# Four heads at a time in 64x64 tiles of TensorE, one ring for all of PSUM, and products of two batches mixed

## The chip, the core and the metric

The kernel runs on one core of a Trainium2 chip. A core has five engines that work side by side, each through its own list of instructions in order: TensorE (PE: matrix products, and the loads of their weights, PEld), VectorE (DVE), ScalarE (ACT), GpSimd (POOL, which here mostly issues loads) and SyncE (SP, which issues stores and transposing copies). They wait for each other through semaphores. TensorE writes its results to PSUM, a memory of eight banks; a bank holds 512 float32 values in each of 128 partitions. ScalarE and VectorE carry them on to SBUF. The time is the device time of one execution in microseconds (us).

## The reference, cut to what matters

Relu-squared attention over 12 heads, then an MLP mixer: a product across tokens, and a two-layer product across channels.

```python
# q, k, v: (8, 12, 448, 64) float32
scores = (1 / 8) * q @ k^T
attn   = maximum(scores, 0) ** 2 / 448 @ v            # (8, 12, 448, 64)
x      = attn as (8, 448, 768)
h      = maximum(x^T @ w_tok1, 0) @ w_tok2            # (448, 256), (256, 448)
u      = x + h^T
h2     = maximum(u @ w_ch1, 0) @ w_ch2                # (768, 1536), (1536, 768)
out    = u + h2                                       # (8, 448, 768) float32
```

## The kernel before

A step works on one pair of heads (48 steps). The heads' 64 channels lie one above the other in 128 partitions, so that a score product uses a 64-row half of the array and a value product a 64-column half. 448 keys are three blocks of 128 and a rest of 64; the two rests of a pair go through one zero-padded 128x128 product. Products with channels are put in a queue and poured between the steps.

```python
ps_att = tile_pool(bufs=2, PSUM)       # two slots of two banks: scores
ps_acc = tile_pool(bufs=1, PSUM)       # one bank: values
ps_mm  = tile_pool(bufs=3, PSUM)       # three banks: everything else

def transposes(s):
    ps = ps_mm.tile([128, 1024], BF16, tag="bank", name="qkT_ps")
    ...                                # 16 transposes: q by 112, k by 128, the rest kz
    nc.vector.tensor_copy(sb, ps[:, : KO + KM + 128])

def scores(s, blocks):
    for c in blocks:
        ps = ps_att.tile([128, 2, 512], FP32, tag="att", name="sc_ps")
        for e in range(2):             # one matmul for each head of the pair
            h = slice(64 * e, 64 * (e + 1))
            nc.tensor.matmul(ps[:, e, :S], lhsT=sb[h, KO + c * 128 : KO + (c + 1) * 128],
                             rhs=sb[h, :S], start=True, stop=True)
    ...                                # relu on ScalarE (at), square on VectorE (sq)

def values(s):                         # 6 matmuls on column halves; values_rest adds one of 128x128
    ...
def values_rest(s):
    ...
    nc.vector.tensor_scalar(out=xT[b % 2][:, p, :S], in0=ps[:, :S], scalar1=float(alpha2), ...)

def token2(s):
    ps = ps_mm.tile([128, 512], FP32, tag="bank", name="h_ps")
    ...                                # 2 matmuls of 448 columns
    nc.vector.tensor_tensor(out=uT_tiles[b // 2][:, p, off : off + S],
                            in0=ps[:, :S], in1=xT[b % 2][:, p, :S], op=ALU.add)

def channel1(b, e):
    ps = ps_mm.tile([128, 512], FP32, tag="bank", name="m1_ps")
    ...                                # 6 matmuls of 448 columns
    nc.scalar.activation(r2[:, e, off : off + S], ps[:, :S], AF.Relu)

def channel2(bb, t, half):
    ps = ps_mm.tile([128, 512], FP32, tag="bank", name="m2_ps")
    for e in range(EC):                # 12 matmuls of 384 columns
        nc.tensor.matmul(ps[:, :HN], lhsT=r2[:, e, tok], rhs=wc2[:, e, cols], ...)
    nc.vector.tensor_tensor(out=o[:, cols], in0=ps[:, :HN], in1=u_tiles[bb][...], op=ALU.add)
    ...                                # after half 1: stores to out

for s in range(NS + 4):
    scores(s, (0, 1)); load_pair(s + 3); ...
    transposes(s + 1)
    values(s - 1)
    scores(s, (2,))
    values_rest(s - 1); ...
    square(); fill(0.25); scores_rest(s); x_back(s - 2); fill(0.25); square()
    ...                                # token2, token1 every second step, fill(0.25) after each
```

`x_back` brings the attention result into token-major order: by transposes on TensorE in the first 12 steps, by a transposing copy afterwards. `token1` is 8 matmuls of 256 columns for two pairs. `fill` pours channel work from the queue, a quarter of a step's share each time.

Of the kernel before, what the change touches and what calls it, by code (L numbers as in the profile page):

```python
# [16 lines left out]
def kernel(  # L17
# [18 lines left out]
    NP = H // 2  # L36
    QC = 4
    QP = S // QC
    KB = 3
    KM = KB * 128  # L40
    KR = S - KM
# [3 lines left out]
    SP = 512  # L45
    HN = DM // 2
    NT = 2 * S // 128

# [4 lines left out]
    raw = ctx.enter_context(tc.tile_pool(name="raw", bufs=6))  # L53
# [3 lines left out]
    ps_att = ctx.enter_context(tc.tile_pool(name="ps_att", bufs=2, space=bass.MemoryType.PSUM))  # L57
    ps_acc = ctx.enter_context(tc.tile_pool(name="ps_acc", bufs=1, space=bass.MemoryType.PSUM))
    ps_mm = ctx.enter_context(tc.tile_pool(name="ps_mm", bufs=3, space=bass.MemoryType.PSUM))
# [4 lines left out]
    kz = [consts.tile([128, NP, 128], BF16, name=f"kz{i}") for i in range(2)]  # L64
    vz = [consts.tile([128, NP, 128], BF16, name=f"vz{i}") for i in range(2)]
    xT = [consts.tile([128, NP, SP], BF16, name=f"xT{i}") for i in range(2)]
# [5 lines left out]


    raws = {}

    def load_pair(s):
        b, p = divmod(s, NP)
        h0 = 2 * p
        q_raw = raw.tile([QP, 2, QC, D], BF16, name="q_raw")
        k_raw = raw.tile([128, 2, KB, D], BF16, name="k_raw")  # L80
        v_raw = raw.tile([128, 2, KB, D], BF16, name="v_raw")
        nc.gpsimd.dma_start(  # L82
            out=q_raw.rearrange("p h c d -> p h (c d)"),
            in_=q[b, h0 : h0 + 2].rearrange("h (p c) d -> p h (c d)", c=QC),
        )
        nc.gpsimd.dma_start(  # L86
            out=k_raw.rearrange("p h c d -> p h (c d)"),
            in_=k[b, h0 : h0 + 2, :KM].rearrange("h (p c) d -> p h (c d)", c=KB),
        )
        if s == 0:  # L90
            make_identity(nc, ident)
        if p == 0:
            load_rest(b, kz[b % 2], k)
        nc.gpsimd.dma_start(  # L94
            out=v_raw.rearrange("p h c d -> p h (c d)"),
            in_=v[b, h0 : h0 + 2, :KM].rearrange("h (p c) d -> p h (c d)", c=KB),
        )
        if p == 0:
            load_rest(b, vz[b % 2], v)
        raws[s] = (q_raw, k_raw, v_raw)  # L100

    def load_rest(b, dst, src):
        for e in range(2):
            nc.gpsimd.dma_start(
                out=dst[64 * e : 64 * e + KR, :, D * e : D * (e + 1)],
                in_=src[b].rearrange("(p e) s d -> e s p d", e=2)[e, KM:],
            )

    def load_wt1():
        w = moe_w_tok1.rearrange("(p c) j -> c p j", c=QC)  # L110
        for c in range(QC):
            lo = c * QP
            while lo < (c + 1) * QP:
                hi = min((c + 1) * QP, (lo // 128 + 1) * 128)
                r = lo % 128
                nc.gpsimd.dma_start(
                    out=wt1[r : r + hi - lo, lo // 128, :],
                    in_=w[c, lo - c * QP : hi - c * QP, :],
                )
                lo = hi  # L120
# [6 lines left out]
    def order_wt2():  # L127
        for j in range(JC):
            nc.vector.tensor_copy(
                wt2[:, j, :].rearrange("n (c p) -> n c p", c=QC),  # L130
                wt2_nat[:, j, :].rearrange("n (p c) -> n c p", c=QC),
            )

    def load_wc1(i):
        n = DC // 2
        nc.gpsimd.dma_start(
            out=wc1[:, :, i * n : (i + 1) * n],
            in_=moe_w_ch1.rearrange("(g p) n -> p g n", p=128)[:, :, i * n : (i + 1) * n],
        )

    def load_wc2(i):
        n = EC // 4
        nc.gpsimd.dma_start(
            out=wc2[:, i * n : (i + 1) * n, :],
            in_=moe_w_ch2.rearrange("(e p) n -> p e n", p=128)[:, i * n : (i + 1) * n, :],
        )


    qkT, at2, squares = {}, {}, []
    KO = S  # L150

    def transposes(s):
        b, p = divmod(s, NP)
        q_raw, k_raw, _ = raws[s]
        ps = ps_mm.tile([128, 1024], BF16, tag="bank", name="qkT_ps")
        blocks = [(c * QP, QP, q_raw[:, :, c, :]) for c in range(QC)]
        blocks += [(KO + c * 128, 128, k_raw[:, :, c, :]) for c in range(KB)]
        blocks.append(
            (KO + KM, 128, kz[b % 2][:, p, :].rearrange("n (h d) -> n h d", h=2))
        )  # L160
        for at, n, src in blocks:
            for h in range(2):
                nc.tensor.matmul(  # L163
                    ps[64 * h : 64 * (h + 1), at : at + n],
                    lhsT=src[:, h, :],
                    rhs=ident[:n, :n],
                    is_transpose=True,
                    start=True,
                    stop=True,
                    skip_group_check=True,  # L170
                )
        sb = attn.tile([128, KO + KM + 128], BF16, name="qkT")
        nc.vector.tensor_copy(sb, ps[:, : KO + KM + 128])  # L173
        qkT[s] = sb

    def relu2(s, key, ps, n):
        at = attn.tile([128, n, S], BF16, tag=f"at{n}", name="at", bufs=3)
        sq = attn.tile([128, n, S], BF16, tag=f"sq{n}", name="sq", bufs=3 * (3 if n == 2 else 1))
        nc.scalar.activation(at, ps[:, :, :S], AF.Relu)  # L179
        squares.append((at, sq))  # L180
        at2[s, key] = sq

    def square():
        for at, sq in squares:
            nc.vector.tensor_tensor(out=sq, in0=at, in1=at, op=ALU.mult)  # L185
        squares.clear()

    def scores(s, blocks):
        sb = qkT[s]
        made = []  # L190
        for c in blocks:
            ps = ps_att.tile([128, 2, 512], FP32, tag="att", name="sc_ps")
            for e in range(2):
                h = slice(64 * e, 64 * (e + 1))
                nc.tensor.matmul(  # L195
                    ps[:, e, :S],
                    lhsT=sb[h, KO + c * 128 : KO + (c + 1) * 128],
                    rhs=sb[h, :S],
                    start=True,
                    stop=True,  # L200
                )
            made.append((c, ps))
        for c, ps in made:
            relu2(s, c, ps, 2)

    def scores_rest(s):
        sb = qkT.pop(s)
        ps = ps_att.tile([128, 1, 512], FP32, tag="att", name="sr_ps")
        nc.tensor.matmul(  # L209
            ps[:, 0, :S],  # L210
            lhsT=sb[:, KO + KM : KO + KM + 128],
            rhs=sb[:, :S],
            start=True,
            stop=True,
        )
        relu2(s, KB, ps, 1)

    accs = {}

    def values(s):  # L220
        v_raw = raws[s][2]
        ps = ps_acc.tile([128, 512], FP32, name="acc_ps")
        for c in range(KB):
            sq = at2.pop((s, c))
            for e in range(2):
                nc.tensor.matmul(  # L226
                    ps[64 * e : 64 * (e + 1), :S],
                    lhsT=v_raw[:, e, c, :],
                    rhs=sq[:, e, :],
                    start=(c == 0),  # L230
                    stop=False,
                    skip_group_check=True,
                )
        accs[s] = ps

    def values_rest(s):
        b, p = divmod(s, NP)
        raws.pop(s)
        ps = accs.pop(s)
        nc.tensor.matmul(  # L240
            ps[:, :S],
            lhsT=vz[b % 2][:, p, :],
            rhs=at2.pop((s, KB))[:, 0, :],
            start=False,
            stop=True,
            skip_group_check=True,
        )
        nc.vector.tensor_scalar(  # L248
            out=xT[b % 2][:, p, :S],
            in0=ps[:, :S],  # L250
            scalar1=float(alpha2),
            scalar2=None,
            op0=ALU.mult,
        )


    x_tiles, r1_tiles, uT_tiles = {}, {}, {}
    PG = 2
    XDMA = 12

    def x_back(s):
        b, p = divmod(s, NP)
        if p % PG == 0:
            x_tiles[s // PG] = mix.tile([128, PG, 4, 128], BF16, name="x_sb")
        if s >= XDMA:
            nc.sync.dma_start_transpose(
                out=x_tiles[s // PG][:, p % PG], in_=xT[b % 2][:, p, :]
            )
            return
# [137 lines left out]
    def fill(share):  # L407
        if not queue:
            return
# [23 lines left out]
    for s in range(NS + 4):  # L433
# [4 lines left out]
        if s == 0:  # L438
            load_wt1()
# [67 lines left out]
```

## Time and profile before

Three runs took 412.56, 412.6 and 415.63 us, median 412.6. The profiled execution spans 411.6 us.

| view | what it says |
|---|---|
| VectorE, ScalarE busy | 216.2 us, 209.5 us |
| channel products, first layer (line 345) | 576 matmuls, 352 ns each as printed |
| channel products, second layer (line 363) | 672 matmuls, 326 ns each as printed |
| relu of a score chunk (line 179) | 144 of 922 ns, ScalarE |
| squares (line 185) | 97.7 us in 192, VectorE |
| granted TensorE clock, mean | 0.983 |

A row of a group reads: line, engine, operation, what is written from what, sizes, count, then busy time and mean of one, then the idle time of the engine just before these instructions and who ended it. A row of a timeline reads: start, length, engine, line, operation, how many in a row, and in brackets the idle time before. Matmuls overlap in the array, so a printed length is longer than the time by which the next one starts later. In the slices of the span, 40 of them, a digit is the busy share in tenths.

### The profile page before, as it was taken

Reading aid. Unit: us, or ns where it says so; the run is one execution under the profiler, and the core shown is the slowest. Engines: PE = TensorE matmul, PEld = TensorE weight load, DVE = VectorE, ACT = ScalarE, POOL = GpSimd, SP = SyncE. Lnnn points to the kernel's source line nnn. Section 1 sums busy time; section 2 is a strip of 40 time slices with the busy share of each in tenths; the row PEclk is TensorE's granted clock in tenths of the full one; section 3 lists DMA queues with packets and bytes.
Section 4 is the critical chain, followed back from the end, with each engine's and each line's share of the span. In section 5 each row is a group of like instructions: output and inputs, shape, how many; then the busy total and the mean of one; then the engine's idle time right before and its main releaser. Section 6 shows DMA issues by size and latency. Waiting matters only on the chain.

```text
span 411.6 us, 7596 instructions
## 1 busy us (share of the span) xinstructions
PE 388.3 (94%) x3033; PEld 205.4 (50%) x3033; DVE 216.2 (53%) x414; ACT 209.5 (51%) x313; POOL 130.8 (32%) x196
## 2 busy tenths in 40 slices
PE   5856799999999999999999999999999999999995
PEld 2323345555445555555445555555545555555562
DVE  2667774466465566365455665356444755432021
ACT  2745676743674446753575347654566237611400
POOL 8995456244243333243223424235222000000000
PEclk9778999999999999999999999999999999999999
DMA  7999999459946999469955989569953434113323
GB/s 75 119 145 203 187 180 196 57 80 126 167 50 69 137 137 143 45 93 134 134 70 56 146 131 147 57 75 134 149 70 47 93 92 92 24 47 99 60 62 93
DMA packets 101572, 43.44 MB, mean 106 GB/s; under 512 B 83424, under 2 KB 97952, under 8 KB 101536
## 3 DMA queue, kind: packets, MB, share of 16 engines
q0 software_dynamic: 54432, 21.70, 50.2%
q1 hardware_dynamic: 47104, 21.25, 25.3%
q8 instruction: 24, 0.39, 0.4%
q14 instruction: 12, 0.10, 0.1%
HBM read 43.38 MB, written 11.01 MB: 132 GB/s over the span
## 4 chain that ended last, share of the span: by engine, by line
PE 85%; DVE 7%; POOL 4%; issue 1%; DMA 1%; ACT 0%; DVEq 0%; ACTq 0%; POOLq 0%
PE m_ps L345 26%; PE m_ps L363 26%; PE sc_ps L195 8%; PE acc_ps L226 6%; PE qkT_ps L163 6%; PE t_ps L290 5%; PE h_ps L308 3%; PE acc_ps L240 3%; DVE sq L185 3%; PE sr_ps L209 2%; DVE uT_sb L316 1%; DMA wt_nat<-in_moe_w_tok_dram 1%; DVE xT L248 1%; POOL k_raw L86 1%; POOL v_raw L94 1%
## 5 line engine op out<-in xcount | busy, mean ns | idle before, releaser
L179 ACT ACTIVATE at<-sc_ps 128x896 bf16<-128x896 f32 x144 | 122.5, 922 | 60.3 <-PE sc_ps L195 59.9
L345 PE MATMUL m_ps<-uT_sb,wc 128*128 128x448 bf16 x576 | 120.3, 352 | 0.6 <-DVE uT_sb L316 0.5
L363 PE MATMUL m_ps<-wc,r_sb 128*128 128x384 bf16 x672 | 116.7, 326 | 0.0
L185 DVE TENSOR_TENSOR sq<-at 128x896 bf16<-128x896 bf16 x192 | 97.7, 559 | 0.1
L94 POOL DMA_DIRECT2D v_raw<-in_v_dram x48 | 34.5, 719 | 170.1 <-PE sc_ps L195 159.3
L363 PEld LDWEIGHTS <-r_sb 128*128 128x128 bf16 x672 | 65.6, 98 | 44.3 <-issue 0.6
L352 ACT ACTIVATE r_sb<-m_ps 128x448 bf16<-128x448 f32 x96 | 52.1, 543 | 65.9 <-PE m_ps L345 65.9
L345 PEld LDWEIGHTS <-wc 128*128 128x128 bf16 x576 | 56.2, 98 | 49.7 <-issue 1.4
L173 DVE COPY qkT<-qkT_ps 128x960 bf16<-128x960 bf16 x48 | 31.5, 656 | 85.6 <-PE qkT_ps L163 85.6
L371 DVE TENSOR_TENSOR out_sb<-m_ps,u_sb 128x384 f32<-128x384 f32 x56 | 31.1, 555 | 71.4 <-PE m_ps L363 69.2
L195 PE MATMUL sc_ps<-qkT 64*128 64x448 bf16 x288 | 45.6, 365 | 2.5 <-ACT at L179 1.3
L248 DVE TENSOR_SCALAR xT<-acc_ps 128x448 bf16<-128x448 f32 x48 | 29.9, 624 | 29.7 <-PE acc_ps L240 29.7
L226 PE MATMUL acc_ps<-sq,v_raw 128*64 128x448 bf16 x288 | 36.7, 363 | 0.0
L82 POOL DMA_DIRECT2D q_raw<-in_q_dram x48 | 33.0, 688 | 10.8 <-DMA wc<-in_moe_w_ch_dram 9.8
L86 POOL DMA_DIRECT2D k_raw<-in_k_dram x48 | 35.2, 732 | 1.7 <-DMA wc<-in_moe_w_ch_dram 1.7
L179 ACT ACTIVATE at<-sr_ps 128x448 bf16<-128x448 f32 x48 | 26.2, 545 | 16.8 <-PE sr_ps L209 16.8
L290 PE MATMUL t_ps<-x_sb,wt 128*128 128x256 bf16 x192 | 25.7, 278 | 9.0 <-DVE x_sb L280 9.0
L298 ACT ACTIVATE r_sb<-t_ps 128x512 bf16<-128x512 f32 x24 | 14.3, 597 | 38.4 <-PE t_ps L290 38.4
L195 PEld LDWEIGHTS <-qkT 64*128 64x128 bf16 x288 | 10.8, 94 | 37.2 <-issue 35.8
L316 DVE TENSOR_TENSOR uT_sb<-h_ps,xT 128x448 bf16<-128x448 f32 x48 | 27.6, 615 | 2.0 <-PE h_ps L308 2.0
L290 PEld LDWEIGHTS <-wt 128*128 128x128 bf16 x192 | 19.0, 99 | 15.0 <-issue 5.1
L163 PEld LDWEIGHTS <-q_raw 112*64 112x64 bf16 x384 | 12.3, 113 | 22.4 <-issue 18.0
(36 smaller groups left out, 209.0 us busy)
## 6 DMA issues: line engine op xcount, KB each, us to landing
q_raw<-in_q_dram POOLq DMA_DIRECT2D x48, 112.0 KB, 3.9
k_raw<-in_k_dram POOLq DMA_DIRECT2D x48, 96.0 KB, 4.2
v_raw<-in_v_dram POOLq DMA_DIRECT2D x48, 96.0 KB, 2.9
out_dram<-out_sb SPq DMA_DIRECT2D x8, 336.0 KB, 2.8
wc<-in_moe_w_ch_dram POOLq DMA_DIRECT2D x2, 1152.0 KB, 12.0
wc<-in_moe_w_ch_dram POOLq DMA_DIRECT2D x4, 576.0 KB, 9.0
out_dram<-out_sb SPq DMA_DIRECT2D x8, 288.0 KB, 2.7
out_dram<-out_sb SPq DMA_DIRECT2D x8, 240.0 KB, 2.8
```

The costliest lines, as they stand in the source:

```text
L86: nc.gpsimd.dma_start(out=k_raw.rearrange("p h c d -> p h (c d)"), in_=k[b, h0 : h0 + 2, :KM].rearrange("h (p c) d -> p h (c d)", c=KB),)
L94: nc.gpsimd.dma_start(out=v_raw.rearrange("p h c d -> p h (c d)"), in_=v[b, h0 : h0 + 2, :KM].rearrange("h (p c) d -> p h (c d)", c=KB),)
L163: nc.tensor.matmul(ps[64 * h : 64 * (h + 1), at : at + n], lhsT=src[:, h, :], rhs=ident[:n, :n], is_transpose=True, start=True, stop=True, ...
L179: nc.scalar.activation(at, ps[:, :, :S], AF.Relu)
L185: nc.vector.tensor_tensor(out=sq, in0=at, in1=at, op=ALU.mult)
L195: nc.tensor.matmul(ps[:, e, :S], lhsT=sb[h, KO + c * 128 : KO + (c + 1) * 128], rhs=sb[h, :S], start=True, stop=True,)
L226: nc.tensor.matmul(ps[64 * e : 64 * (e + 1), :S], lhsT=v_raw[:, e, c, :], rhs=sq[:, e, :], start=(c == 0), stop=False, skip_group_check=True,)
L248: nc.vector.tensor_scalar(out=xT[b % 2][:, p, :S], in0=ps[:, :S], scalar1=float(alpha2), scalar2=None, op0=ALU.mult,)
L290: nc.tensor.matmul(ps[:, j, :], lhsT=wt1[:, c, j * 128 : (j + 1) * 128], rhs=x_sb[:, :, c, :], start=(c == 0), stop=(c == 3),)
L345: nc.tensor.matmul(ps[:, :S], lhsT=wc1[:, g, e * 128 : (e + 1) * 128], rhs=uT[:, g, off : off + S], start=(g == 0), stop=(g == CC - 1),)
L352: nc.scalar.activation(r2[:, e, off : off + S], ps[:, :S], AF.Relu)
L363: nc.tensor.matmul(ps[:, :HN], lhsT=r2[:, e, tok], rhs=wc2[:, e, cols], start=(e == 0), stop=(e == EC - 1), skip_group_check=True,)
```

## The change

A step now works on four heads. Head dimensions and key chunks are both 64, so that scores and values each use four 64x64 tiles of the array in turn; 448 keys are seven chunks of 64 and nothing is padded. Tokens are taken in seven interleaved sets of 64 (`(p c)`, c = 7), which gives one row of 1792 bytes in a load. All of PSUM is one ring of four slots of two banks each; every kind of product takes the next slot, and two-bank tiles let one evacuation carry twice the width. The score chunks of all steps form one stream, three to a group (a "burst"), so groups run across the borders of steps. First-layer channel products of one batch are mixed with second-layer products of the batch before. It is meant to use the array better, to make fewer and larger evacuations, and to even out the load of the engines.

```diff
-    ps_att = ctx.enter_context(tc.tile_pool(name="ps_att", bufs=2, space=bass.MemoryType.PSUM))
-    ps_acc = ctx.enter_context(tc.tile_pool(name="ps_acc", bufs=1, space=bass.MemoryType.PSUM))
-    ps_mm = ctx.enter_context(tc.tile_pool(name="ps_mm", bufs=3, space=bass.MemoryType.PSUM))
+    psum = ctx.enter_context(tc.tile_pool(name="psum", bufs=4, space=bass.MemoryType.PSUM))
...
+    def bank2(shape, dtype, name):
+        return psum.tile(shape, dtype, tag="slot", name=name)
...
+    def scores(s, c):
+        sb = qkT[s]
+        ps = bank2([128, 2, 512], FP32, "sc_ps")
+        for half in range(2):
+            for e in range(2):
+                rows = slice(64 * e, 64 * (e + 1))
+                nc.tensor.matmul(
+                    ps[64 * half : 64 * (half + 1), e, :S],
+                    lhsT=sb[rows, 0, half, c, :],
+                    rhs=sb[rows, 1, half, :, :],
...
+        sq = attn.tile([128, 2, S], BF16, name="sq", bufs=13)
+        nc.scalar.activation(sq, ps[:, :, :S], AF.Relu)
...
+    def values(s):
+        v_raw = raws.pop((s, "v"))
+        ps = bank2([128, 2, 512], FP32, "acc_ps")
+        for c in range(KC):
...
+        nc.vector.tensor_scalar(
+            out=xTs[s % XB][:, :, :S],
+            in0=ps[:, :, :S],
...
+    def token2(s):
...
+        ps = bank2([128, 2, 512], FP32, "h_ps")
...
         nc.vector.tensor_tensor(
-            out=uT_tiles[b // 2][:, p, off : off + S],
-            in0=ps[:, :S],
-            in1=xT[b % 2][:, p, :S],
+            out=uTs[b // 2][:, 2 * i : 2 * i + 2, off : off + S],
+            in0=ps[:, :, :S],
+            in1=xTs[s % XB][:, :, :S],
...
+    def channel1(b, e0):
+        ps = bank2([128, 2, 512], FP32, "m1_ps")
+        for i in range(2):
+            for g in range(CC):
...
+        nc.scalar.activation(r2[:, e0 : e0 + 2, off : off + S], ps[:, :, :S], AF.Relu)
...
+    def channel2(bb, t):
+        ps = bank2([128, 2, 512], FP32, "m2_ps")
+        for i in range(2):
+            cols = slice(i * HN, (i + 1) * HN)
+            for e in range(EC):
+                nc.tensor.matmul(
+                    ps[:, i, :HN],
+                    lhsT=r2[:, e, tok],
+                    rhs=wc2[:, e, cols],
...
+            nc.vector.tensor_tensor(
+                out=o[:, cols].rearrange("n (g d) -> n g d", d=128),
+                in0=ps[:, i, :HN].rearrange("n (g d) -> n g d", d=128),
...
+    def refill():
+        if order or not early:
+            return
+        firsts = early[: EC // 2]
+        del early[: EC // 2]
+        seconds = late.pop(0) if len(late) > 1 else []
...
+    SB = 3
+    tiles = [(s, c) for s in range(NS) for c in range(KC)]
+    n_bursts = len(tiles) // SB
...
+    PERIOD = 4000.0
+    for s in range(NS):
+        first, last = (KC * s) // SB, (KC * s + KC - 1) // SB
+        if s > 0:
+            at(first - 2, lambda s=s: transposes(s))
+        at(last + 1, lambda s=s: x_back(s))
+    transposes(0)
+    for kb in range(n_bursts + 6):
+        for s, c in tiles[kb * SB : (kb + 1) * SB]:
+            scores(s, c)
...
+                values(s)
...
         square()
+        for f in todo.get(kb, []):
+            f()
+        fill(0.5 * PERIOD)
...
+                token1(s)
...
+                token2(s)
+        fill(0.5 * PERIOD)
```

A first-layer unit is now two banks wide (12 matmuls, one relu of 896), a second-layer unit is both halves of a token tile (24 matmuls, two additions). `fill` takes 4000 ns of channel work per burst. The x transposes on TensorE are for the first 9 steps of four heads. The reordering of `w_tok2` moves from VectorE to GpSimd, and squares are made in place.

## The prediction

> **What bounds the kernel now.** I read the page from the top: the busy shares, the slices, the chain that ended last. Then the timeline of TensorE in the middle and at the end, because what the change costs is decided by who waits for whom inside one step.
>
> ```profile
> PE 388.3 (94%) x3033; PEld 205.4 (50%) x3033; DVE 216.2 (53%) x414; ACT 209.5 (51%) x313; POOL 130.8 (32%) x196
> PE   5856799999999999999999999999999999999995
> ...
> PE 85%; DVE 7%; POOL 4%; issue 1%; DMA 1%; ACT 0%; DVEq 0%; ACTq 0%; POOLq 0%
> ```
>
> TensorE carries 85% of the chain; from about 60 us on every slice is at 9. Before that it has only attention to do, and waits. ScalarE and VectorE are half busy. In the steady part the timeline of TensorE has no hole:
>
> ```profile
> 204.15 1.30 PE L345 MATMUL m_ps<-uT_sb,wc 128*128 128x448 bf16 x6
> 205.38 0.55 PE L195 MATMUL sc_ps<-qkT 64*128 64x448 bf16 x4
> 205.86 0.39 PE L163 MATMUL qkT_ps<-ident,q_raw 112*64 112x112 bf16 x8
> 206.08 0.34 PE L163 MATMUL qkT_ps<-ident,k_raw 128*64 128x128 bf16 x6
> 206.25 0.22 PE L163 MATMUL qkT_ps<-ident,kz 128*64 128x128 bf16 x2
> 206.31 0.73 PE L226 MATMUL acc_ps<-sq,v_raw 128*64 128x448 bf16 x6
> 206.97 0.36 PE L195 MATMUL sc_ps<-qkT 64*128 64x448 bf16 x2
> 207.27 0.36 PE L240 MATMUL acc_ps<-sq,vz 128*128 128x448 bf16 x1
> 207.47 1.30 PE L345 MATMUL m_ps<-uT_sb,wc 128*128 128x448 bf16 x6
> 208.60 0.35 PE L209 MATMUL sr_ps<-qkT 128*128 128x448 bf16 x1
> 208.79 1.30 PE L345 MATMUL m_ps<-uT_sb,wc 128*128 128x448 bf16 x6
> ```
>
> The differences of the starts are the real costs, since the printed ends overlap. Attention of one pair takes 0.48 (two score chunks) + 0.45 (transposes) + 0.66 (values) + 0.30 + 0.20 + 0.19 = 2.28 us. Six channel matmuls take about 1.13 us, so 189 ns each at 448 columns. Four score matmuls on two row halves take two such times, so the halves do run at once; two column halves do too (values: six in 0.66 us). At the end of the kernel the channel output runs without a hole as well, while VectorE adds beside it:
>
> ```profile
> 395.70 10.89 PE L363 MATMUL m_ps<-wc,r_sb 128*128 128x384 bf16 x66
> ```
>
> ```profile
> 406.63 0.56 DVE L371 TENSOR_TENSOR out_sb<-m_ps,u_sb 128x384 f32<-128x384 f32 x1 [1.39 <-PE m_ps L363]
> ```
>
> From the same timelines: a consumer starts 0.20 us after TensorE's slot ends (207.47 to the xT scaling at 207.67), and TensorE resumes some 0.06 us after a consumer's end. The durations that I use:
>
> ```profile
> L179 ACT ACTIVATE at<-sc_ps 128x896 bf16<-128x896 f32 x144 | 122.5, 922 | 60.3 <-PE sc_ps L195 59.9
> L371 DVE TENSOR_TENSOR out_sb<-m_ps,u_sb 128x384 f32<-128x384 f32 x56 | 31.1, 555 | 71.4 <-PE m_ps L363 69.2
> L316 DVE TENSOR_TENSOR uT_sb<-h_ps,xT 128x448 bf16<-128x448 f32 x48 | 27.6, 615 | 2.0 <-PE h_ps L308 2.0
> ```
>
> TensorE's work before: 48 pairs x 2.28 = 109.4; token products 24 x (0.87 + 0.76) = 39.1; x transposes 12 x 0.3 = 3.6; channel products 576 x 0.189 + 672 x 0.163 = 218.4. Sum 370.5 us of the span of 411.6, so 41 us idle or slow, most of it before the first channel product at 58 us.
>
> [...] the row halves run at once, and a group next to another mode costs about 0.1 us more than its matmuls (0.48 against 0.38). [...] In the kernel before each channel product has its own one-bank tile[...]. Four tiles at once, two by two, no run here shows; I take it from the two halves of each kind.
>
> **The change, part by part.**
>
> *Four tiles at once.* For four heads: 7 score chunks x 0.189 = 1.32, 7 value chunks the same (they follow scores in the same mode), 28 transposes in 14 pairs x 0.056 = 0.78; changes of mode 0.1 in each group. 56 bursts of three chunks x 0.667 = 37.4, values 24 x 1.32 = 31.8, transposes 24 x 0.88 = 21.1: 90.3 us against 109.4. The x transposes grow from 12 to 18 pairs (5.0 against 3.6). Token and channel products stay. TensorE's work becomes 352.6 us, **18 us less**.
>
> *The ring.* Each product of any kind now takes the next of four slots, and must wait until the slot's tenant of four places before is drained. A burst takes three slots in 0.67 us; the product after it takes the slot of the one that stood just before the burst. Where that was a channel1 pair, ScalarE needs 0.20 + 0.92 + 0.06 = 1.18 us, so 0.51 us are left over beyond the burst; token2 (896 elements, about 1.08 by the slope of 615 ns at 448): 0.67; token1 0.20; channel2's second half 0.15. In the built order, bursts 18 to 55 follow a channel1 pair 16 times, channel2 12, token1 7 and token2 3 times: 8 + 2 + 1.5 + 2 = **14 us**. Three steps where bursts nearly touch ("burst, transposes, token1, burst") wait for relus and squares, 1.5 to 2 us each: 5.5. In this stretch the first channel1 of three batches waits for the one big token2 addition that gives it its last input, 0.20 + 1.08 + 0.06, 1.4 each: 4.2. Together **24 us**.
>
> *Channel2 as one two-bank tile.* Both halves are now in one tile, and the addition of the first half is recorded before the matmuls of the second. In the built program the second half's first matmul waits on VectorE; counting completions, what it waits for is that addition. The banks differ, but the guard is by tile. So in each of the 28 tiles TensorE stands 0.20 + 0.56 + 0.06 = 0.82 us: **23 us**. In some ten of them VectorE still has squares or the qkT copy (about 1.1 us at 1792) ahead of it in its fixed order: some **7 us** more. Before, this addition lay beside the next half's matmuls.
>
> *Start and thin stretch.* Channel products start after burst 10. Followed by hand, a pair of early bursts costs about 9.2 us, bound by VectorE (six squares of 0.6, scaling, x copy, qkT copy, addition) and the ring; the tenth burst comes at 44 us, with 23 us of TensorE's work done: 21 idle (before: 29 by 58 us). The second-layer products of batch 0 are now held back until batch 1 is there, so bursts 14 to 16 have no channel work; bursts 10 to 17 take 50 us for 35 us of work: **15 idle**. What is held back is done after the last burst, in a dense tail. End: 5 us as now, 1.5 for the last token addition.
>
> *Loads* become rows of 1792 bytes in place of 768 and 1024, 144 issues in place of 176: good for the crowded first 36 us, nothing later.
>
> Sum: 352.6 + 21 + 15 + 24 + 30 + 6.5 = 449 us. I shade it to **440**, because waits that I added up overlap: a stop inside channel2 lets ScalarE and VectorE catch up, and the next wait shrinks.
>
> **Rivals.** (1) The gain stands and the waits don't: TensorE runs ahead by slots, and the start is shorter by 10 us; that gives 385 to 395. For it: half-empty ScalarE and VectorE, and the shorter list of work. Against it: TensorE takes its instructions in order, and its waits at a drained slot are each longer than the work in between. (2) Only the halves of channel2 cost, the ring is wide enough: 411.6 - 18 + 23 to 30, so 417 to 424. For it: average slot use is far below four slots' capacity. Against: three slots are taken within 0.67 us, faster than one relu of 0.92. (3) Four tiles don't run at once, only two: scores and values cost twice, + 64 us, 500. Against it: both halvings work in the trace. (4) VectorE becomes the bound: its sum is about as before, 220 us, so only in the early bursts.
>
> **Range and chances.** The 18 us of gain and the 23 us of the halves are firm; the ring and the early stretch are worth 20 to 60 us by hand and are the spread. 8 in 10: 418 to 458. Faster than 404 needs nearly all waits to be absent: 0.05. Within 2%: 0.11. Slower: 0.84.
>
> **What would show it.** TensorE's idle time at channel2 with the VectorE addition as releaser, 23 to 30 us, and holes of 0.8 us every 1.95 us in the tail; holes of some 0.5 us after bursts, released by channel1's relu; one batch, seven bursts, in 48 to 51 us against 46.4 (t_ps at 203.44 and 249.84 in the chain); the first channel product near 46 to 48 us. I am wrong if channel2 shows no such holes, if a chunk of four score matmuls takes clearly more than 0.19 us, or if TensorE's idle time in the middle is under 15 us.

## The result

The changed kernel takes 467.2 us (465.5 to 469.3), the kernel before 413.1 us beside it. The ratio is 1.130, 95% interval 1.125 to 1.134: 13% slower. The forecast was 440 us, range 418 to 458. The direction was right, the size too small, and the time lies outside the range.

The page of the changed kernel, the same rows as for the kernel before: busy shares, the slices of TensorE, the chain that ended last.

```profile
PE 390.6 (84%) x3633; PEld 214.2 (46%) x3633; DVE 209.9 (45%) x310; ACT 198.0 (42%) x242; POOL 94.8 (20%) x161
...
PE   5677787788987988979998798897988898998985
...
PE 67%; DVE 15%; ACT 10%; issue 5%; POOL 1%; DMA 1%; ACTq 0%; DVEq 0%; POOLq 0%
```

TensorE has fallen from 85% to 67% of the chain. VectorE's 15% and ScalarE's 10% are not there because these engines have more to do (209.9 and 198.0 us of work against 216.2 and 209.5), but because TensorE now stops for them. The slices after 60 us, nearly all nines before, are now a mix of 7, 8 and 9. TensorE's timeline in the middle (start, length, line, operation, count, and in brackets the idle time with its releaser):

```profile
229.09 2.11 PE L303 MATMUL m_ps<-wc,r_sb 128*128 128x384 bf16 x12
231.86 2.11 PE L303 MATMUL m_ps<-wc,r_sb 128*128 128x384 bf16 x12 [0.65 <-DVE out_sb L310]
233.90 0.76 PE L157 MATMUL sc_ps<-qkT 64*64 64x448 bf16 x12
234.62 1.52 PE L185 MATMUL acc_ps<-sq,v_raw 64*64 64x448 bf16 x28
236.06 0.58 PE L133 MATMUL qkT_ps<-ident,k_raw 128*64 128x128 bf16 x14
236.48 0.56 PE L133 MATMUL qkT_ps<-ident,q_raw 128*64 128x128 bf16 x14
236.97 1.05 PE L232 MATMUL t_ps<-x_sb,wt 128*128 128x256 bf16 x8
237.85 2.43 PE L286 MATMUL m_ps<-uT_sb,wc 128*128 128x448 bf16 x12
240.22 0.76 PE L157 MATMUL sc_ps<-qkT 64*64 64x448 bf16 x12
241.29 2.43 PE L286 MATMUL m_ps<-uT_sb,wc 128*128 128x448 bf16 x12 [0.31 <-ACT r_sb L293]
```

Four tiles do run at once: twelve score matmuls from 233.90 to 234.62 are 0.72 us, three times 0.19 and a rest; 28 value matmuls take 1.44 us. And both predicted holes are there: in the middle of channel2 (231.86), and after a burst that follows channel1 (241.29). The printed hole is 0.17 us shorter than the real one, because the printed end of a matmul lies that much after its slot; by the starts the first is 231.86 - 229.09 - 12 x 0.163 = 0.81 us. The tail, where the kernel before ran 66 matmuls without a stop:

```profile
440.01 4.06 PE L303 MATMUL m_ps<-wc,r_sb 128*128 128x384 bf16 x24 [0.65 <-DVE out_sb L310]
444.72 4.06 PE L303 MATMUL m_ps<-wc,r_sb 128*128 128x384 bf16 x24 [0.65 <-DVE out_sb L310]
449.43 4.06 PE L303 MATMUL m_ps<-wc,r_sb 128*128 128x384 bf16 x24 [0.65 <-DVE out_sb L310]
```

The 24 here are the second half of one tile and the first of the next, so there is one stop to a tile. The list of waits (total us, times, longest) names the three largest of TensorE:

```profile
PE m_ps L303 <- DVE out_sb L310: 23.4, 28, 1.5
PE m_ps L286 <- DVE uT_sb L258: 15.3, 8, 2.5
PE x_ps L215 <- DVE xT L193: 10.8, 9, 1.2
```

By the starts these three are 27.9, 16.6 and 12.5 us. Waits after bursts are spread over many rows and come to 15 to 20 us by the starts, without or with some 0.1 us at each burst for the change of tile shape (an estimate, from the 0.48 us of the score group in the kernel before against 0.38 for its matmuls). The second row is the one that I had badly sized. Six of its eight waits are long (printed 2.2 to 2.5 us, 2.3 to 2.7 by the starts; the first is printed with 1.2, the last with 0.4). In the kernel before, the same place cost next to nothing:

```profile
PE m_ps L345 <- DVE uT_sb L316: 0.5, 3, 0.2
```

All engines around one of the six:

```profile
255.25 0.93 PE L250 MATMUL h_ps<-wt,r_sb 128*128 128x448 bf16 x4
255.37 1.09 DVE L193 TENSOR_SCALAR xT<-acc_ps 128x896 bf16<-128x896 f32 x1 [1.62 <-PE acc_ps L185]
...
256.02 0.92 PE L286 MATMUL m_ps<-uT_sb,wc 128*128 128x448 bf16 x4
256.38 1.69 DVE L174 TENSOR_TENSOR sq<-sq 128x896 bf16<-128x896 bf16 x3
...
257.98 1.08 DVE L258 TENSOR_TENSOR uT_sb<-h_ps,xT 128x896 bf16<-128x896 f32 x1
259.12 1.35 PE L286 MATMUL m_ps<-uT_sb,wc 128*128 128x448 bf16 x5 [2.18 <-DVE uT_sb L258]
```

Token2's product is done at 256.0, but its addition starts at 257.98: VectorE takes its list in order, and the scaling of the values and three squares stand ahead. TensorE has begun the new batch's first channel product with the four inputs that it has (256.02, x4), and stands at its head for the last two. The same place in TensorE's own timeline shows something more:

```profile
259.12 2.47 PE L286 MATMUL m_ps<-uT_sb,wc 128*128 128x448 bf16 x8 [2.18 <-DVE uT_sb L258]
261.52 1.34 PE L157 MATMUL sc_ps<-qkT 64*64 64x448 bf16 x12
```

Eight matmuls take 2.40 us in place of 1.51, and a burst 1.27 in place of 0.72: the granted clock is at one half (0.51 on the mean from 259.8 to 263.2 us). Five of the six long waits are followed by such a stretch of 3.41 us. This one costs 0.89 us in the eight matmuls, 0.55 in the burst and 0.22 in the twelve behind it (2.49 us in place of 2.27), 1.66 us in all; my estimate for the five is thus some 8 us.

### The profile page after: what moved, and what is told of

It reads as the page before. It is cut to its first block, busy times and chain, and to the rows that moved or that the text cites. A ratio compares the mean times of both kernels' runs of the same rounds, so it can differ in the third digit from the quotient of the medians.

```text
span 466.0 us, 8554 instructions
## 1 busy us (share of the span) xinstructions
PE 390.6 (84%) x3633; PEld 214.2 (46%) x3633; DVE 209.9 (45%) x310; ACT 198.0 (42%) x242; POOL 94.8 (20%) x161
## 4 chain that ended last, share of the span: by engine, by line
PE 67%; DVE 15%; ACT 10%; issue 5%; POOL 1%; DMA 1%; ACTq 0%; DVEq 0%; POOLq 0%
PE m_ps L286 24%; PE m_ps L303 22%; PE acc_ps L185 8%; ACT sq L166 7%; PE t_ps L232 4%; DVE out_sb L310 3%; PE sc_ps L157 3%; DVE sq L174 3%; DVE xT L193 3%; PE h_ps L250 3%; DVE uT_sb L258 3%; PE qkT_ps L133 3%; ACT r_sb L293 2%; DVE qkT L146 2%; PE x_ps L215 1%
## 5 line engine op out<-in xcount | busy, mean ns | idle before, releaser
L166 ACT ACTIVATE sq<-sc_ps 128x896 bf16<-128x896 f32 x168 | 141.9, 929 | 76.1 <-PE sc_ps L157 76.1
L303 PE MATMUL m_ps<-wc,r_sb 128*128 128x384 bf16 x672 | 117.6, 326 | 24.3 <-DVE out_sb L310 23.4
L286 PE MATMUL m_ps<-uT_sb,wc 128*128 128x448 bf16 x576 | 123.0, 364 | 16.7 <-DVE uT_sb L258 15.3
L174 DVE TENSOR_TENSOR sq<-sq 128x896 bf16<-128x896 bf16 x168 | 100.3, 622 | 66.6 <-ACT sq L166 66.1
L293 ACT ACTIVATE r_sb<-m_ps 128x896 bf16<-128x896 f32 x48 | 44.0, 917 | 125.6 <-PE m_ps L286 124.8
L81 POOL DMA_DIRECT2D v_raw<-in_v_dram x48 | 28.7, 605 | 216.2 <-PE acc_ps L185 212.7
L157 PE MATMUL sc_ps<-qkT 64*64 64x448 bf16 x672 | 50.0, 388 | 5.2 <-ACT sq L166 1.9
L193 DVE TENSOR_SCALAR xT<-acc_ps 128x896 bf16<-128x896 f32 x24 | 26.2, 1092 | 56.6 <-PE acc_ps L185 56.6
L185 PE MATMUL acc_ps<-sq,v_raw 64*64 64x448 bf16 x672 | 36.6, 353 | 5.4 <-ACT r_sb L293 2.2
L185 PEld LDWEIGHTS <-v_raw 64*64 64x64 bf16 x672 | 23.0, 107 | 18.7 <-issue 11.9
L258 DVE TENSOR_TENSOR uT_sb<-h_ps,xT 128x896 bf16<-128x896 f32 x24 | 26.1, 1088 | 6.8 <-PE h_ps L250 6.8
L146 DVE COPY qkT<-qkT_ps 128x1792 bf16<-128x1792 bf16 x23 | 24.9, 1083 | 0.0
L250 PE MATMUL h_ps<-wt,r_sb 128*128 128x448 bf16 x96 | 22.2, 354 | 0.0
```

The source lines that it names most:

```text
L81: nc.gpsimd.dma_start(out=r[64 * half : 64 * (half + 1)], in_=src[b, h0 : h0 + 2].rearrange("e (p c) d -> p e (c d)", c=KC),)
L157: nc.tensor.matmul(ps[64 * half : 64 * (half + 1), e, :S], lhsT=sb[rows, 0, half, c, :], rhs=sb[rows, 1, half, :, :], start=True, stop=Tru ...
L166: nc.scalar.activation(sq, ps[:, :, :S], AF.Relu)
L174: nc.vector.tensor_tensor(out=sq, in0=sq, in1=sq, op=ALU.mult)
L185: nc.tensor.matmul(ps[64 * e : 64 * (e + 1), half, :S], lhsT=v_raw[rows, e, c * D : (c + 1) * D], rhs=sq[rows, e, :], start=(c == 0), stop ...
L193: nc.vector.tensor_scalar(out=xTs[s % XB][:, :, :S], in0=ps[:, :, :S], scalar1=float(alpha2), scalar2=None, op0=ALU.mult,)
```

## The experiments

My theory: the time is lost at single places on TensorE's list, where it stops for another engine although its next instruction does not need what it waits for, or need not stand there. The rivals: the ring of four slots as a whole sets the pace, so a wait that is removed reappears; or what is lost is hidden time, and several repairs together bring less than their sum. All expectations below were written before the runs.

**Both additions after both halves of channel2.**

```diff
             for e in range(EC):
                 nc.tensor.matmul(ps[:, i, :HN], ...)
+        for i in range(2):
+            cols = slice(i * HN, (i + 1) * HN)
             nc.vector.tensor_tensor(out=o[:, cols]..., in0=ps[:, i, :HN]..., ...)
```

> Both VectorE additions of a channel2 tile are recorded after its 24 matmuls, so that the second half no longer waits for the addition out of the first half; all else as in the changed kernel (467.2 us). My theory: the 28 waits in the middle (23.4 us of idle time in the changed kernel's profile, 28 x 0.8 to 1.6 us by the starts) go, and some 5 us come back because the slot is drained later (0.20 + 2 x 0.56 + 0.06 = 1.4 us after the last matmul, beyond a burst of 0.72, in the 12 places where a burst follows channel2): 440 to 449 us. Rival, the ring sets the pace anyway and the wait only changes its place: above 460 us.

Measured: 441.8 us (441.6 to 443.0), ratio to the kernel before 1.069 (1.064 to 1.073): 25.5 us less. Its waits:

```profile
PE m_ps L286 <- DVE uT_sb L258: 14.3, 7, 2.5
...
PE acc_ps L185 <- DVE out_sb L312: 3.0, 6, 0.5
```

The row with 28 waits is gone, and as expected a little comes back: values and other products now wait for the later drain of the slot, 5.3 us in three rows. The long waits for the token addition stay, but in this trace only two half-clock stretches lie between 40 us and the end of TensorE's work, in place of five; by the estimate above that is 5 of the 25.5 us. The other 20 or so are the stop in channel2: real cost, not time that another limit would have taken.

**A slot of its own for each half.**

```diff
-        ps = bank2([128, 2, 512], FP32, "m2_ps")
         for i in range(2):
+            ps = bank2([128, 512], FP32, "m2_ps")
             cols = slice(i * HN, (i + 1) * HN)
```

> Each half of a channel2 tile takes a slot of the ring of its own, with its addition beside the next half as in the kernel before; the ring turns faster, by 28 slots in all. My theory, that the guard by tile is the cost: the waits in the middle go as well, the drain after the last half stays at 0.82 us; 437 to 447 us. Rival, four slots are too few and a fifth taker in a row has to wait for its predecessors: 455 us or more, with the idle time moved to the score matmuls and to the first matmul of channel2, released by relus.

Measured: 438.0 us (436.3 to 438.8), ratio 1.058 (1.054 to 1.062): 29.3 us less, close to the prediction's 23 + 7 (three half-clock stretches past 40 us are left in this trace, so some 3 us of it are the clock's). The ring turns faster and no new wait of note comes of it. It is 3.8 us better than the run before, where the slot was drained after two additions and not one: the 5.3 us of waits for that drain are gone from the list. The guard is by tile: the halves lie in two banks in both versions, the same addition runs beside the same matmuls, and with two tiles the row of 28 stops (23.4 us) is gone.

**The new batch's channel products one burst later.**

```diff
         if i == GS - 1:
-            channel_work(b)
+            pending.append(b)
...
         square()
+        while pending:
+            channel_work(pending.pop(0))
```

> Channel products of a batch join the queue one burst later, after the next burst's scores, so that the first of them no longer stands at the head of TensorE's list while the last token addition waits behind three squares on VectorE. My theory: the 8 waits of 2.2 to 2.7 us (15.3 us idle, some 17 by the starts) shrink to under 3 us in all, and the stretches at half the granted clock that begin in them (five of 3.4 us, at about 91, 208, 259, 317 and 368 us of the span, 1.2 to 1.7 us lost each) go with them: 443 to 452 us, mean clock back above 0.98. Rival, TensorE has nothing else to do there and the time is lost in the next burst: 460 us or more; second rival, the half clock has another cause: clock stays near 0.97.

Measured: 454.0 us (452.9 to 454.4), ratio 1.097 (1.093 to 1.101): 13.3 us less, 2 us short of the expectation.

```profile
PE m_ps L303 <- DVE out_sb L310: 26.7, 28, 1.5
...
PE m_ps L286 <- DVE uT_sb L258: 3.0, 5, 0.7
```

The wait falls from 15.3 to 3.0 us, no half-clock stretch is left between the first 30 us and the end of TensorE's work, and the mean clock is 0.984 (0.969 in the changed kernel). So in these two traces the half clock comes with these waits. Waits and clock together had cost some 25 us, yet 13.3 are won. Most of the rest went into other stops: 26.7 in place of 23.4 us in channel2, 3.4 in place of 1.9 where scores wait for relus, and 1.9 where first-layer products wait for the relu of a score chunk, a row that is not in the changed kernel's list. My written account was wrong in two things: not all eight waits are that long, and the slow stretches do not begin in the wait but 0.2 to 1.3 us after its end.

**Groups of two chunks.**

```diff
-    SB = 3
+    SB = 2
-    PERIOD = 4000.0
+    PERIOD = 4000.0 * 2 / 3
```

> Score chunks in groups of two in place of three (84 bursts of two, channel credit 2667 ns for each), so the product after a burst takes a slot that was given back one product earlier. My theory: the waits after bursts for the drain of channel1 (some 0.5 us each, 16 of them, 8 us) go, 28 more changes of tiling mode cost 0.1 us each, 3 us; the waits inside channel2 stay: 455 to 464 us. Rival, the ring costs nothing and the longer chain of bursts only adds changes of mode and later tokens: 468 to 475 us.

Measured: 449.2 us (448.8 to 453.2), ratio 1.088 (1.082 to 1.094): 18 us less, more than any account had said.

```profile
PE m_ps L303 <- DVE out_sb L310: 24.7, 28, 1.4
...
PE m_ps L286 <- DVE uT_sb L258: 9.1, 7, 1.6
```

The waits after bursts did shrink, by some 6 us by the starts. What I had not seen is the second row: with two squares ahead of it and not three, the token addition comes sooner, and the first channel1's wait falls from 15.3 to 9.1 us; the clock stays up (0.989), with no half-clock stretch between 45 us and the end. These 6.2 us and the estimated 8 of the clock are most of the gain: the same cost as in the run before, by another door. As a test of the ring it is confounded.

**No mixing of batches.**

```diff
-        firsts = early[: EC // 2]
+        order.extend(early[: EC // 2] + late.pop(0))
         del early[: EC // 2]
-        seconds = late.pop(0) if len(late) > 1 else []
-        ...
```

> Channel products of two batches are not mixed: after the first-layer products of a batch come the second-layer products of the same batch, as in the kernel before. My theory: holding back the second layer leaves bursts 14 to 16 of the changed kernel without channel work (from 74 to 89 us of its span TensorE stands for some 5 us) and again less dense stretches at the end of each batch; undoing it gives 6 to 12 us: 455 to 461 us, with a tail of pure channel work that is some 12 us shorter. Rival, the mixing evens out ScalarE and VectorE, and without it runs of channel1 wait for relus: 467 to 475 us.

Measured: 462.9 us (462.1 to 463.5), ratio 1.119 (1.115 to 1.123): 4.3 us less, the direction but not the size. Even this is not shown to be the mixing's: this trace has two half-clock stretches past 40 us in place of five, by the estimate above some 5 us, as much as the gain. What the run does show is that the mixing brings no gain worth naming here.

**x transposes one burst later.**

```diff
-        at(last + 1, lambda s=s: x_back(s))
+        at(last + 2, lambda s=s: x_back(s))
...
-            if last + (2 if s < XDMA else 3) == kb:
+            if last + 3 == kb:
                 token1(s)
-            if last + (3 if s < XDMA else 4) == kb:
+            if last + 4 == kb:
                 token2(s)
```

> The x transposes on TensorE, and the token products behind them, come one burst later for the first nine steps, so that they do not stand right behind the value products and wait for the scaling out of PSUM. My theory: nine waits of 1.2 us shown (13.5 us by the starts) go, but six of the nine lie in the early stretch where VectorE and the loads also set the pace, so half to two thirds of it is won: 458 to 462 us. Rival, the early stretch is bound by VectorE alone and the wait only moves: 465 us or more.

Measured: 462.6 us (461.9 to 466.8), ratio 1.120 (1.114 to 1.127): 4.7 us less of the 12.5 that stood there by the starts (I had put it at 13.5). Almost two thirds of this wait was not worth anything: TensorE now waits 4.0 us for loads of k (0.7 in the changed kernel) and 25.2 us in channel2 (23.4).

**Three repairs together** (own slot, later channel products, later x):

> Three repairs together: a slot for each half of channel2, channel products of a new batch one burst later, x transposes one burst later. If the costs are separate places on TensorE's list they add: 467.2 - 29.3 - 13.3 - 7 = 418 us, 413 to 422. If they hide each other, less is won: 424 us or more.

Measured: 416.0 us (414.2 to 417.2), ratio 1.006 (1.004 to 1.008). The single gains are 29.3 + 13.3 + 4.7 = 47.3 us, together 51.3. They add, and a little more, so the repairs do not hide each other. That is not to say that each wait was worth its length: by the starts the three rows and the slow clock had come to 27.9 + 16.6 + 8 + 12.5 = 65 us.

**All, with groups of two and no mixing:**

> As the run with three repairs, and also groups of two score chunks and no mixing of batches. Of the 18 us that groups of two gave alone, some 11 came through the first channel1 of a batch, which is repaired already, so 5 to 7 are left; no mixing gives 6 to 10: 400 to 408 us, under the kernel before (413.7). Rival, without the large waits the ring of four slots becomes the bound, and the four-tile products cannot bring it under the kernel before: 414 us or more.

Measured: 405.2, 408.2, 409.6 and 413.7 us, median 408.9; ratio 0.986 (0.979 to 0.992). The ratios of this run and the next leave out executions more than 1.5% above the fastest of their version. At the upper edge of the expected span, under the kernel before.

**The same, batches still mixed:**

> The three repairs and groups of two score chunks, batches still mixed: parts the two things that differ between the run with three repairs (416.0 us) and the run with all (408.9). If groups of two bring it by freeing the ring, 409 to 412 us; if the mixing was the cost, 414 to 417 us, as with three repairs alone.

Measured: 405.6, 411.4, 412.9 and 416.1 us, median 412.2; ratio 0.987 (0.978 to 0.996), from the two lowest. The spread covers both answers, so it does not part groups of two from mixing. The profiled execution, of 412.9 us, shows where such time goes: TensorE waits 7.8 us in all for four transposing copies of x, which land 3.0 to 10.3 us after their issue, and one of these waits, 4.85 us long, is followed by 6.8 us of half clock.

**Later token products where x comes by copy** (in the version with all):

```diff
-            if last + 3 == kb:
+            if last + (3 if s < XDMA else 4) == kb:
                 token1(s)
-            if last + 4 == kb:
+            if last + (4 if s < XDMA else 5) == kb:
                 token2(s)
```

> As the run with all repairs, with the token products one burst later for the steps whose x comes by transposing copy: in that run TensorE waited 2 us once and 0.7 us once for such a copy, and its times spread from 405 to 414 us. If these copies cause the spread, the highest run falls under 410 us and the median to 404 to 407 us; if not, nothing moves: 408 to 410 us.

Measured: 405.8 us, from 405.3 to 405.9; ratio 0.980 (0.977 to 0.983). The spread is gone, and so are the waits for transposing copies, though these still land 3.1 to 8.3 us after their issue. With the trace of the run before, this speaks for copies that land late as the cause of the spread; the executions of 408 us and more of the version with all were not traced, so for them it is inferred from four runs of each. The best execution is not better than before (405.2 there).

**And the x copies ahead of the squares:**

```diff
-        at(last + 2, lambda s=s: x_back(s))
+        xs.setdefault(last + 2, []).append(s)
...
+        for s in xs.get(kb, []):
+            x_back(s)
         square()
```

> As the run before it, and the x copies of the first nine steps are put ahead of the squares on VectorE, since in the early stretch token1 waited 2.1, 1.3 and 0.7 us for a copy that stood behind them: 4 us less if that is where the time goes, 401 to 404 us; no gain, 405 us or more, if the squares behind the copy only delay the values by as much.

Measured: 404.8 us (404.6 to 405.0), ratio 0.978 (0.976 to 0.980). One microsecond, at the edge of what can be told from the run before. TensorE's waits for these copies fall from 4.1 to 0.5 us, but those for loads of q rise from 1.9 to 3.5 and those of scores for qkT from 0.5 to 1.9. It is the fastest version: 2.2% under the kernel before. Its busy shares and slices:

```profile
PE 378.1 (94%) x3633; PEld 205.7 (51%) x3633; DVE 208.9 (52%) x310; ACT 199.3 (49%) x242; POOL 95.4 (24%) x161
...
PE   6877899999999999989999989999999989998995
```

The work is that of the changed kernel, instruction for instruction on TensorE (3633 matmuls); only the order and the slots differ, and from 50 us on the slices are nearly all nines.

**The guard put back** in this version (the two halves of channel2 in one tile again):

```diff
+        ps = bank2([128, 2, 512], FP32, "m2_ps")
         for i in range(2):
-            ps = bank2([128, 512], FP32, "m2_ps")
```

> The best version with the two halves of channel2 put back into one tile, with the first half's addition ahead of the second half's matmuls. If the wait is a cost of its own on TensorE's list, whatever stands around it: 404.8 + 25 to 30 = 430 to 435 us, slower than the kernel before. If it mattered only because the changed kernel was full of holes: under 420 us.

Measured: 433.5 us (432.8 to 435.8), ratio 1.049 (1.046 to 1.052): 28.7 us more. The 28 stops are back (24.4 us as printed), and neither trace has a half-clock stretch between 47 us and the end, so this is the cleanest measure of the guard. Where the tile is taken decides between 2% faster than the kernel before and 5% slower, in a kernel with few other holes as in one full of them.

## Why the prediction was right and where it failed

**What bounds the kernel, and the direction.** Right. TensorE was the bound, the change shortened its work and lengthened the span by making it stop.

**Four tiles at once.** The mechanism held; the gain was over-sized. By the starts four heads take 7/3 x 0.72 + 1.44 + 0.91 = 4.03 us against 4.56, so 24 x 0.53 = 13 us, less 1.4 for the x transposes: some 11 us, where the prediction had 18. The term "bursts of three chunks x 0.667" measures 0.72, and the values' 1.32 measures 1.44. The rival "only two run at once" is refuted by the same rows.

**Channel2 as one tile.** Right in place, mechanism and size: 23 + 7 us predicted, 27.9 measured by the starts (28 stops of 0.82 and some 5 us more in seven that are longer, where ten were forecast), 29.3 by taking it out and 28.7 by putting it back.

**The ring.** The waits after bursts came where they were listed and as long as said (printed 0.31 after channel1, with the 0.17 that is 0.48, against 0.51). In all 15 to 20 us against 14 plus 5.5. No run of mine isolates the ring's worth: groups of two changed other things with it.

**The first channel1 of a batch. This is the step that failed.** The prediction had "0.20 + 1.08 + 0.06, 1.4 each: 4.2", for three batches, as if VectorE were free when the token product ends. It is not: scaling and three squares stand ahead in its order, the wait is 2.3 to 2.7 us by the starts at six of the eight batches, and shorter at the first and last, 16.6 us together. In addition the clock falls to one half after five of the six, some 8 us, which was not in the sum. That makes 25 us against 4.2. I had counted such a queue for channel2 and forgot it here. Taking the wait out gave 13.3 us: with this step alone repaired the kernel takes 454.0 us, inside the range that was forecast.

**Start and thin stretch.** Right: the tenth burst started at 43.4 us (said: 44), the first channel product at 47.6 (46 to 48), and bursts 10 to 17 took 51.6 us (50).

**Loads.** "Good for the crowded first 36 us" is not shown: over the whole run the median time from issue to landing went up, for q from 3.9 to 5.4 us at the same 112 KB.

**The shade.** The unshaded sum was 449 us; I took 9 off because "waits that I added up overlap". With the failed step and the gain at their measured sizes (+21, +7) the unshaded sum would be 477, ten above the measured 467, so a discount of about this size was due. Its reason was seen too: with the waits for the token addition gone, the stops of channel2 grew by 3.3 us, and the nine x waits of 12.5 us were worth 4.7. A batch took (365.72 - 204.61) / 3 = 53.7 us by the first channel products of three batches, outside the 48 to 51 that I had named.

**The rivals.** That only the halves cost, 417 to 424 us, fails: without them it is still 438. That the gain stands and the waits don't, 385 to 395, fails for the kernel as it is, but not as an idea: with the stops taken out the four-tile design comes to 404.8, faster than the kernel before.

**Still open:** how the 11 us between the version with three repairs and the fastest are shared between groups of two, mixing and distance to the copies. The traces point to the groups: by the starts, what TensorE loses after bursts past 46 us is 22.3 us with three repairs, 16.6 with all, and 16.0 with the same except that batches stay mixed. That is a reading, not a test.

## What to carry to other kernels

The wider tiles made fewer evacuations (24 token additions in place of 48), but the guard went by tile: where the addition out of one half was recorded ahead of the matmuls into the other, TensorE stopped for it, although the halves lie in two banks (28 stops, 23.4 us as printed, 27.9 by the starts). Look for a releaser that reads the very tile which is waited for. When sizing a wait for an engine, do not take its instruction's duration alone, but everything that stands ahead of it in that engine's list. And do not take the length of a wait for what its removal wins: here 27.9 us of waits gave 29.3, but 25 gave 13.3 and 12.5 gave 4.7. The gains themselves did add.

## What the runs showed that I had not expected

TensorE's clock falls to one half for 3.41 us after waits that are printed with 2.2 to 2.5 us: at 92.6, 208.6, 259.8, 317.9 and 369.1 us of the changed kernel's span (mean granted clock 0.50 to 0.51 in the 3.4 us from there), each 0.2 to 1.3 us after the wait's end, though not after every such wait (one of 2.5 us, at 146 to 149 us, has none: the clock is 1.00 from 146 to 150 us).

The length of the wait does not set the sixth apart. In the 3.41 us just before the five stretches TensorE has 2.66, 2.34, 2.34, 2.07 and 2.34 us without a matmul by the starts, and the sixth wait has 2.65 us. What decides in this trace whether the clock cost of such a wait is paid is not shown. The run with both additions last and the run with a slot for each half kept these waits (14.3 and 14.1 us) and have two and three half-clock stretches past 40 us in place of five. In the run that removes the waits (3.0 us left, the longest 0.7) none of these stretches is left.
